# Block-sparse attention with a SwiGLU layer: the loads of batches 1 to 3 on GpSimd's queue, the first query tile on ScalarE, mask columns in two pieces

## The chip, the cores and the metric

The kernel runs on one core of a Trainium2 chip. The metric is the device time of one execution in microseconds (us). A separate execution is taken with the hardware profiler; its page and its trace are what is read here. On the page PE is TensorE's matmul, PEld its weight load, DVE is VectorE, ACT ScalarE, POOL GpSimd and SP SyncE; a letter q behind a name means the engine's sequencer, which waits and issues DMAs. PS is the PSUM tile with its eight banks.

## The reference

Attention over 4 batches, 8 heads, 768 positions and head size 64, with a mask on blocks of 32 positions, followed by a normalised SwiGLU layer on the 3072 x 512 result:

```python
scores = scale * np.matmul(q, k.transpose(0, 1, 3, 2))
mask = np.abs(blk_i - blk_j) <= window          # window = 1
mask = mask | (blk_i == 0) | (blk_j == 0) | (blk_i == n_blocks - 1) | (blk_j == n_blocks - 1)
# and three sampled key blocks for each query block
scores = np.where(mask, scores, -1000000000.0)
attn = softmax(scores)
attn_out = np.matmul(attn, v)
x = attn_out.transpose(0, 2, 1, 3).reshape(B * S, H * D)
rms = np.sqrt(np.mean(x * x, axis=-1, keepdims=True) + 1e-06)
xn = x / rms * rms_g
g = xn @ w_gate                                 # 512 x 1536
silu = g * (1.0 / (1.0 + np.exp(-g)))
val = xn @ w_val
return silu * val @ w_out                       # 1536 x 512
```

Inputs and output are float32.

## The kernel before

**Pairs of heads.** Two heads of one batch are a pair; there are 16 pairs, numbered g, four to a batch. For a pair, k, q and v are loaded as float32, 128 partitions x 2 heads x 384 elements (384 KB each), into a tile `qkv` of which there are three (`raw`). `fill` casts k and q to bf16 into `aug`, 64 columns of each row, beside 24 columns that hold the mask: the keys' block indicator, and for queries the mask row of the query's block. One matmul over 88 rows thus gives scores and mask together. `pad_v` casts v into `vaug`, and with that the pair's `raw` buffer is free again. The transposed form of `aug` goes to `XA`, with five slots: for the four pairs of batch 0 by TensorE (`tpx`, evicted by `evx`), for all later pairs by a DMA transpose, `turn` (L241), from one of two `aug` buffers.

**Units.** The work on queries comes in ten units: three single tiles of 128 queries and one of three tiles for batch 0, then two of three tiles for each further batch. A unit runs QK (`qk`, L272), the exponential on ScalarE (`exp`, L292), AV (`av`, L306), normalisation (`xo`), the sum of squares (`sq`), its reciprocal root on GpSimd (`rsq`, L339), the scaled row (`xq`, L346) and its transpose, by TensorE for the first three units and by a DMA transpose (`xt`, L372) for the others. Then follow gate and value products (`proj`, L384), tanh (`th`, L393), `uu` (L399) and `hp` (L410) on VectorE, and the output product (`yy`, L423), with its eviction `yo` (L433) and the store. While attention of one unit runs, products of an earlier one are put between its matmuls.

**Order.** A planner at the end of the kernel writes all engines' orders. Each step is an `op` with a price for every engine that could run it, its dependences, its priority and the buffers that it takes and gives back. The planner takes in turn the step that could start first by its own clock. Two resources, `DMA` and `DMA2`, stand for SyncE's and ScalarE's queues; a landing is put some time after the issue (8.0 for a load of batches 1 to 3). The engines then run these orders as they stand, each in order, and wait on semaphores.

**Transfers.** Loads of batch 0 are issued at the start, on SyncE's queue except for the first 64 columns of q, which go on ScalarE's. The weights are read as float32 and written as bf16 by DMAs on GpSimd's queue (`load_w`, L207, eight of 128 x 4 x 384; `load_wo`, L211, two of 128 x 6 x 512), behind a small copy that waits for v of pair 1 (`gate_pool`). The loads of batches 1 to 3 are on SyncE's queue, as are the transposes and the stores. Ahead of the loads of pairs 4 to 7, SyncE issues a read of two elements out of a weight tile into `scr` (`gate_sync`, L217); it has to wait until that weight DMA has landed, and what stands behind it in SyncE's order waits too.

**The first query tile.** GpSimd casts the first 64 columns of q for both heads into `aug[0]` (`fillq(0, 0, 1)`), and ScalarE copies all mask columns for queries out of PSUM (L187).

Of the kernel before, what the change touches and what calls it, by code (L numbers as in the profile page):

```python
# [10 lines left out]
BF16 = mybir.dt.bfloat16  # L11
# [6 lines left out]
def kernel(  # L18
# [12 lines left out]
    nc = tc.nc  # L31
    SIMOUT = None
    P = 128
    B, H, S, D = q.shape
    NB = S // 32
    NC = S // P
    DM = H * D
    DFF = moe_w_gate.shape[1]
    NF = DFF // P
    NP = H // 2  # L40
# [3 lines left out]
    KQ = D + NB  # L44
# [12 lines left out]
    const = ctx.enter_context(tc.tile_pool(name="const", bufs=1))  # L57
# [8 lines left out]
    qv = q.rearrange("b h (p c) d -> b p h (c d)", c=NC)  # L66
    kv = k.rearrange("b h (p c) d -> b p h (c d)", c=NC)
    vv = v.rearrange("b h (p c) d -> b p h (c d)", c=NC)

    raws = {}  # L70
    aug = [const.tile([P, 2, 2, NC, P], BF16, name=f"aug{i}") for i in range(NAUG)]
# [4 lines left out]
    def load(g, i):  # L76
        b, pr = divmod(g, NP)
        if i == 0:
            raws[g] = raw.tile([P, 3, 2, NC * D], FP32, name="qkv", tag="qkv")
        nc.sync.dma_start(out=raws[g][:, i], in_=(kv, qv, vv)[i][b, :, 2 * pr:2 * pr + 2, :])  # L80

    TI = work.tile([P, DM], I32, name="ti", tag="yo", bufs=3)
    TF = work.tile([P, DM], FP32, name="tf", tag="yo", bufs=3)
# [6 lines left out]
    A = [raw.tile([P, 3, 2, NC * D], FP32, name="qkv", tag="qkv") for g in range(3)]  # L90
# [9 lines left out]
    load0(1, 0)  # L100
    load0(1, 1)
    gB = const.tile([P, DM], FP32, name="gB")
    scr = const.tile([P, 16], BF16, name="scr")
    scf = const.tile([P, 1], FP32, name="scf")

    def copy(eng, out, in_):
# [19 lines left out]
    def idle(n, bk=7):  # L126
# [7 lines left out]
        out=kmask, in_=kmask, compare_op=ALU.is_ge, fill=0.0,  # L134
        base=0, pattern=[[1, NC], [-32, NB]], channel_multiplier=NC)
    nc.gpsimd.affine_select(
        out=kmask, in_=kmask, compare_op=ALU.is_ge, fill=0.0,
        base=31, pattern=[[-1, NC], [32, NB]], channel_multiplier=-NC)
    nc.gpsimd.affine_select(
        out=ident, in_=ident, compare_op=ALU.not_equal, fill=1.0,  # L140
        base=0, pattern=[[-1, P]], channel_multiplier=1)
    nc.gpsimd.affine_select(
        out=Bm, in_=Bm, compare_op=ALU.is_ge, fill=0.0,
        base=1, pattern=[[-1, 32]], channel_multiplier=1)
    nc.gpsimd.affine_select(
        out=Bm, in_=Bm, compare_op=ALU.is_ge, fill=0.0,
        base=1, pattern=[[1, 32]], channel_multiplier=-1)
    nc.gpsimd.affine_select(
        out=Bm, in_=Bm, compare_op=ALU.not_equal, fill=1.0,
# [13 lines left out]
    for t in aug:  # L163
# [7 lines left out]
        out=eq[0:NB], in0=jb[0:NB], in1=samp_f[0:NB].unsqueeze(2).to_broadcast([NB, NRND, 32]),  # L171
        op=ALU.is_equal)
# [3 lines left out]
    for r in range(NRND):  # L176
        nc.vector.tensor_tensor(
            out=Bm[0:NB], in0=Bm[0:NB], in1=eq[0:NB, r], op=ALU.max)
    nc.vector.tensor_scalar(
        out=Bneg, in0=Bm, scalar1=-MASKV, scalar2=MASKV, op0=ALU.mult, op1=ALU.add)  # L180
    qm = PS[:, 2, 0:NC * NB].rearrange("p (c j) -> p c j", j=NB)
    for c in range(NC):
        nc.tensor.matmul(  # L183
            out=qm[:, c, :], lhsT=Kind[0:NB, c, :], rhs=Bneg[0:NB, 0:NB], start=True, stop=True)
    idle(WARM[2])

    nc.scalar.copy(out=aug[0][:, 1, :, :, D:KQ], in_=qm.unsqueeze(1).to_broadcast([P, 2, NC, NB]))  # L187

    def fillk(g, eng, e=slice(0, 2)):
        copy(eng, aug[g % NAUG][:, 0, e, :, 0:D],  # L190
# [6 lines left out]
    wv = const.tile([P, DM // P, DFF], BF16, name="wv")  # L197
    wo = const.tile([P, NF, DM], BF16, name="wo")
# [3 lines left out]
    NWC, NOC = 4, 2  # L202
    FW, FO = DFF // NWC, NF // NOC
# [6 lines left out]
    def load_wo(i):  # L210
        nc.gpsimd.dma_start(  # L211
            out=wo[:, i * FO:(i + 1) * FO, :], in_=wov[:, i * FO:(i + 1) * FO, :])

    def gate_sync(n):
        f0 = n * FW if n < NWC else (n - NWC) * FO * DM
        src = wv[0:1, 0, f0:f0 + 2] if n < NWC else wo[0:1, (n - NWC) * FO, 0:2]
        nc.sync.dma_start(out=scr[0:1, 2 * n:2 * n + 2], in_=src)  # L217

    def fillq(g, lo, hi, eng):
        src = A[g][:, 1, :, lo * D:hi * D] if lo < 3 else tiles["q2"][:, 2 * g:2 * g + 2, :]  # L220
        copy(eng, aug[g % NAUG][:, 1, :, lo:hi, 0:D], src.rearrange("p e (c d) -> p e c d", d=D))
# [232 lines left out]
    def op(key, engs, deps, prio, fn, acq=(), rel=(), at=0.0):  # L454
        o = dict(key=key, engs=engs, deps=deps, prio=prio, fn=fn, acq=acq, rel=rel, at=at,
                 n=len(ops))
        ops.append(o)
        made[key] = o
# [12 lines left out]
        "p (i e x) -> p i e x", i=3, e=2))  # L471

    ld0(("l", 0, 0), 1.2)
    op(("l", 0, 1, 0), {"DMA2": 0.3}, [], (0,), None)
    ld0(("l", 0, 1, 1), 0.35)
    ld0(("l", 1, 0), 1.0)
    ld0(("l", 1, 1), 0.6)
    for g, i in ((2, 0), (2, 1), (3, 0), (3, 1), (0, 2), (1, 2), (2, 2), (3, 2)):
        ld0(("l", g, i), 0.6 if i == 1 else 1.1,
            lambda e, p, g=g, i=i: load0(g, i))  # L480
    ld0(("lg",), 0.7, lambda e, p: nc.sync.dma_start(
        out=gB, in_=moe_rms_g.unsqueeze(0).to_broadcast([P, DM])))
# [31 lines left out]
    for g in range(NP):  # L514
        a_ = g % NAUG
        rr = [("raw", g)] if g < NP - 1 else []
        if g:
            op(("fk", g), {"DVE": 0.57, "POOL": 0.84}, [("l", g, 0)], (-1, g, 0),
               lambda e, p, g=g: fillk(g, e), [(f"aK{a_}", g)], rr)
        for n_, (es, lo, hi) in enumerate(QP[g == 0]):  # L520
            dep = ("q2",) if lo == 3 else ("l", 0, 1, n_) if g == 0 else ("l", g, 1)
            pri = (-1, g, 1) if lo == 0 else (2.5, g, lo)
            fe = {"DVE": 0.09 + 0.085 * (hi - lo), "POOL": 0.1 + 0.13 * (hi - lo)}
            op(("fq", g, lo), {"POOL": 0.25} if g == 0 and lo == 0 else fe, [dep] + [("m1",)] * (g == 1 and lo == 0), pri,
               lambda e, p, a=(g, lo, hi): fillq(*a, e), [(f"a{'QR'[lo == 3]}{a_}", (g, lo == 3))],
               rr if lo < 3 else [("hp", ("q2",))])
        for i in range(2):
            for n_, (es, lo, hi) in enumerate((KP, QP)[i][g == 0]):
                m_ = len(es) * (hi - lo)
                if i == 0:  # L530
                    pri = (-1, g, 0.5 + 0.1 * n_ + (g == 0 and lo == 3))
                else:
                    pri = (-1, g, 1) if lo == 0 else (2.5, g, lo)
                res = f"aK{a_}" if i == 0 else f"a{'QR'[lo == 3]}{a_}"
                key = ("tp", g, i, es[0], lo)
                op(key, {"PE": m_ * 0.056}, [("fq", g, lo)] if i else [("fk", g)] if g else [],
                   pri, lambda e, p, a=(g, i, es, lo, hi): tpx(*a, p),
                   [(TP1[:2] if i and lo == 3 else TP1, key), (f"X{g}", g)],
                   [(res, g)] if i == 0 else [(res, (g, lo == 3))])
                de = {"DVE": 0.07 + m_ * P / 1560.0}  # L540
                ac = {"ACT": 0.15 + m_ * P / 1200.0}
                if g == 0 and i == 0:
                    de = (de, de, {**de, **ac})[n_]
                elif g == 0 and lo == 0:
                    de.update(ac)
                op(("ev",) + key[1:], de, [key], pri,
                   lambda e, p, a=(g, i, es, lo, hi): evx(*a, e), [], [(None, key)])
        op(("pv", g), {"DVE": 0.57, "POOL": 1.0}, [("l", g, 2)], (0, g, 2),
           lambda e, p, g=g: pad_v(g, e), [("va0", 0)], rr)
# [7 lines left out]
    for g in range(NP, B * NP):  # L557
        b, pr = divmod(g, NP)
        gate = {NP: 2, NP + 1: 3, NP + 2: 4, NP + 3: 5}.get(g)
        for i in range(3):  # L560
            def ld(e, p, g=g, i=i, gate=gate):
                if gate is not None and i == 0:
                    gate_sync(gate)
                load(g, i)
            op(("ld", g, i), {"DMA": 1.1}, [("w", gate)] if gate is not None and i == 0 else [],
               (1,), ld, [("raw", g)] if i == 0 else [])
            if i < 2:
                op(("fill", g, i), {"DVE": 0.57}, [("ld", g, i), ("zp", 0), ("zp", 1)] + [
                    ("tp", g_, i_, 0, 3 * i_) for g_ in (2, 3) for i_ in range(2)],
                   (4, g, i), lambda e, p, g=g, i=i: fill(g, i, e), [(f"aug{g % NAUG}", (g, False))])  # L570
            else:
                op(("pv", g), {"DVE": 0.57}, [("ld", g, 2), ("fill", g, 0), ("fill", g, 1)],
                   (4, g, 2), lambda e, p, g=g: pad_v(g, e), [(f"va{b % 2}", b)], [("raw", g)])
        op(("turn", g), {"DMA": 4.6}, [("fill", g, 0), ("fill", g, 1)], (-1, g),
           lambda e, p, g=g: turn(g), [(f"X{g % NSLOT}", g)], [(f"aug{g % NAUG}", (g, False))])
# [11 lines left out]
    for u, (b, c0, nt) in enumerate(UNITS):  # L587
# [32 lines left out]
        if u < NPET:  # L620
            op(("tr", u), {"PE": nt * NP * 0.056}, [("xq", u, t) for t in range(nt)], (0, u),
               lambda e, p, u=u: tr(u, p), [(TP1 if nt < 3 else S_, ("tr", u)), ("xn", u)], [("xq", u)])
            op(("cp", u), {"ACT": 0.15 + nt * DM / 1200.0, "DVE": 0.17 + nt * DM / 1950.0}, [("tr", u)], (0, u),
               lambda e, p, u=u: cp(u, e), [], [(None, ("tr", u))])
        else:
            op(("cp", u), {"DMA": 1.8}, [("xq", u, t) for t in range(nt)], (-2, u),
               lambda e, p, u=u: xt(u), [("xn", u)], [("xq", u)])
        fg = FG[nt]
        w_of = [-(-(f + 1) * fg * P // FW) - 1 for f in range(NF // fg)]
# [25 lines left out]
                op(("yo", u, t, h), {"ACT": 0.15 + DM / nh / 1200, "DVE": 0.16 + DM / nh / 960}, [("y", u, t, 4 * h + 3)], (5, u, t),  # L655
                   lambda e, p, a=(u, t, h): yo(*a, e), [], [(None, ("y", u, t, h))])

    free = {"PE": 4.7, "ACT": 4.98, "DVE": 4.7, "POOL": 3.2, "DMA": 2.1, "DMA2": 2.3}
    left = {o["key"]: len(o["deps"]) for o in ops}
    users = {}  # L660
    for o in ops:
# [37 lines left out]
    while ready:  # L699
# [22 lines left out]
        _, o, e, t1, got = pick  # L722
# [73 lines left out]
```

The softmax here doesn't subtract the row's maximum and nothing guards it: scores larger than these inputs give would overflow.

## Time and profile before

| What | Value |
|---|---|
| Median of 3 runs | 309.65 us (309.52 to 312.66) |
| The profiled execution's own time | 309.14 us |
| Its span, first to last instruction | 307.4 us |
| TensorE busy | 299.2 us, 97% |
| ScalarE busy | 202.4 us, 66% |
| VectorE busy | 192.1 us, 62% |
| GpSimd busy | 25.1 us, 8% |
| DMA on SyncE's queue | 37.56 MB, 48.9% of 16 engines' span |
| DMA on GpSimd's queue | 4.72 MB (as written), 9.9% |
| Loads of k, q, v: issue to landing, median | 5.5, 6.0, 5.6 us |
| Weights: wg, wv, wo, the same | 7.1, 8.2, 18.4 us |
| DMA transposes to XA and xn, the same | 6.5, 4.4 us |

Busy time of TensorE is modelled from the starts of its matmuls. A group's line has its source line, engine and operation, output and inputs by the program's names, the count, the busy time and the mean, and the idle time of the engine just before it with what ended most of that. A line of the waits has who waited for whom, the total, the count and the longest. A line of a timeline has the start and the length in us.

### The profile page before, as it was taken

What the parts mean: (1) busy time and instruction counts of PE and PEld (TensorE: products, weight loads), DVE (VectorE), ACT (ScalarE), POOL (GpSimd) and SP (SyncE); (2) the same over time, 40 slices, a digit from 0 to 9 for tenths busy, and PEclk for the clock granted to TensorE, in tenths of its full rate; (3) what the DMA queues carried; (4) which work ended last, traced back from release to release, by engine and by line L of the source; (5) the groups of instructions that cost most, each with busy time, mean ns of one, the idle gap of its engine ahead of it and who ended that gap; (6) DMA issues with size and microseconds to landing.
All of it is one profiled execution on the core that took longest, in us unless ns stands there. A gap on an engine that the chain in (4) does not pass through costs nothing.

```text
span 307.4 us, 7325 instructions
## 1 busy us (share of the span) xinstructions
PE 299.2 (97%) x3022; PEld 199.6 (65%) x3050; DVE 192.1 (62%) x434; ACT 202.4 (66%) x317; POOL 25.1 (8%) x44
## 2 busy tenths in 40 slices
PE   8999999989999999999999999999999999999995
PEld 7898888746667566666666666666666556556543
DVE  6778766855779768756754754663499617627500
ACT  4999875676887888777778787888723223333221
POOL 4566000100000001001000100010001000000000
PEclk9999999999999999999999999999999999999999
DMA  7999999999999899940793050003100140020022
GB/s 213 365 224 190 225 277 214 225 301 275 264 272 249 229 208 267 267 151 16 148 189 81 0 87 2 34 3 85 36 0 2 23 132 2 11 91 2 0 104 104
DMA packets 72230, 42.82 MB, mean 139 GB/s; under 512 B 49924, under 2 KB 69124, under 8 KB 72196
## 3 DMA queue, kind: packets, MB, share of 16 engines
q1 hardware_dynamic: 66096, 37.56, 48.9%
q0 software_dynamic: 5792, 4.72, 9.9%
q8 instruction: 24, 0.39, 0.5%
q10 hardware_dynamic: 308, 0.07, 0.1%
q14 instruction: 10, 0.08, 0.1%
HBM read 28.57 MB, written 6.29 MB: 113 GB/s over the span
## 4 chain that ended last, share of the span: by engine, by line
PE 95%; ACT 2%; DMA 2%; issue 1%; DVE 0%; ACTq 0%
PE PS L384 41%; PE PS L272 19%; PE PS L423 19%; PE PS L306 12%; PE PS L254 2%; DMA xn<-xq 2%; ACT pt L292 1%; PE PS L128 1%; PE PS L153 0%; PE PS L357 0%; ACT yo L433 0%; PE PS L183 0%; DVE zt L115 0%; ACTq L433 0%
## 5 line engine op out<-in xcount | busy, mean ns | idle before, releaser
L292 ACT ACTIVATE pt<-PS 128x768 bf16<-128x768 f32 x188 | 142.9, 812 | 33.7 <-PE PS L272 33.2
L399 DVE SCALAR_TENSOR_TENSOR uu<-th,PS 128x384 bf16<-128x384 bf16 x96 | 53.1, 554 | 61.7 <-ACT th L393 58.8
L272 PE MATMUL PS<-XA 88*128 88x384 bf16 (+1 forms) x480 | 81.7, 294 | 0.6 <-ACT pt L292 0.6
L384 PE MATMUL PS<-xn,wg 128*128 128x384 bf16 (+1 forms) x480 | 75.2, 294 | 1.2 <-DMA xn<-xq 1.2
L384 PE MATMUL PS<-xn,wv 128*128 128x384 bf16 (+1 forms) x480 | 75.3, 293 | 0.0
L393 ACT ACTIVATE th<-PS 128x384 bf16<-128x384 f32 x96 | 47.3, 493 | 38.1 <-PE PS L384 35.4
L423 PE MATMUL PS<-wo,hp 128*128 128x512 bf16 (+1 forms) x272 | 65.5, 370 | 1.5
L410 DVE TENSOR_TENSOR hp<-uu,PS 128x384 bf16<-128x384 bf16 x96 | 51.4, 551 | 15.2 <-PE PS L384 14.6
L384 PEld LDWEIGHTS <-wg 128*128 128x128 bf16 x480 | 41.4, 98 | 23.9 <-issue 1.6
L384 PEld LDWEIGHTS <-wv 128*128 128x128 bf16 x480 | 41.6, 97 | 23.4
L272 PEld LDWEIGHTS <-XA 88*128 88x128 bf16 x480 | 39.4, 98 | 21.3 <-issue 1.6
L423 PEld LDWEIGHTS <-hp 128*128 128x128 bf16 x300 | 29.0, 98 | 26.8
L306 PEld LDWEIGHTS <-pt 128*128 128x128 bf16 x1128 | 40.5, 97 | 5.7
L306 PE MATMUL PS<-vaug,pt 128*128 128x65 bf16 x1128 | 42.1, 193 | 0.0
L433 ACT ACTIVATE yo<-PS 128x512 f32<-128x512 f32 (+1 forms) x23 | 13.3, 580 | 26.4 <-PE PS L423 25.7
L339 POOL TENSOR_TENSOR rs<-ms,nhalf 128x3 f32<-128x3 f32 (+1 forms) x10 | 7.9, 786 | 204.0 <-DVE ms L331 163.7
L318 DVE TENSOR_TENSOR xo<-PS,rz 128x384 f32<-128x384 f32 (+1 forms) x40 | 19.1, 477 | 1.4
L346 DVE SCALAR_TENSOR_TENSOR xq<-xo,rs,gB 128x512 bf16<-128x512 f32 x24 | 17.5, 748 | 3.3 <-POOL rs L339 3.3
L331 DVE CUSTOM_DVE_ANT_0 sc<-xo 128x512 bf16<-128x512 f32 (+1 forms) x24 | 16.3, 680 | 0.2
L112 DVE CAST aug<-qkv 128x768 bf16<-128x768 f32 (+1 forms) x28 | 14.5, 538 | 0.1
L317 DVE RECIPROCAL rz<-PS 128x6 f32<-128x6 f32 (+1 forms) x40 | 7.4, 186 | 8.1 <-PE PS L306 7.8
L112 DVE COPY XA<-PS 88x768 bf16<-88x768 bf16 (+2 forms) x17 | 8.5, 518 | 2.7 <-PE PS L254 2.7
(59 smaller groups left out, 71.2 us busy)
## 6 DMA issues: line engine op xcount, KB each, us to landing
out_dram<-yo SPq DMA_DIRECT2D x23, 256.0 KB, 2.2
qkv<-in_v_dram SPq DMA_DIRECT2D x15, 384.0 KB, 5.6
qkv<-in_k_dram SPq DMA_DIRECT2D x14, 384.0 KB, 5.5
qkv<-in_q_dram SPq DMA_DIRECT2D x12, 384.0 KB, 6.0
wg<-in_moe_w_gate_dram POOLq DMA_DIRECT2D x4, 384.0 KB, 7.1
wv<-in_moe_w_val_dram POOLq DMA_DIRECT2D x4, 384.0 KB, 8.2
wo<-in_moe_w_out_dram POOLq DMA_DIRECT2D x2, 768.0 KB, 18.4
q<-in_q_dram SPq DMA_DIRECT2D x1, 768.0 KB
```

The lines of the kernel that those rows point to most:

```text
L112: nc.vector.tensor_copy(out=out, in_=in_)
L272: nc.tensor.matmul(out=s_[:, e, j * w:(j + 1) * w], lhsT=x[0:KQ, 0, e, jt * P:(jt + 1) * P], rhs=x[0:KQ, 1, e, c0 * P:c0 * P + w], start=T ...
L292: nc.scalar.activation(out=pts[u, pr][:, g * kt:(g + 1) * kt].rearrange("p j e w -> p e j w"), in_=s_[:, :, 0:kt * w].rearrange("p e (j w) ...
L306: nc.tensor.matmul(out=o_[:, t, e, :], lhsT=pt[:, jt, e, t * P:(t + 1) * P], rhs=va[:, (2 * pr + e) * NC + jt, 0:D + 1], start=(jt == 0), ...
L318: nc.vector.tensor_tensor(out=xos[u][:, :, 2 * pr:2 * pr + 2, :], in0=o_[:, :, :, 0:D], in1=rz.unsqueeze(3).to_broadcast([P, nt, 2, D]), o ...
L331: nc.vector.tensor_tensor_reduce(out=sc[:, z], in0=x, in1=x, scale=1.0 / DM, scalar=mss[u][:, 0:1] if nt == 1 and t else 1e-6, op0=ALU.mul ...
L346: nc.vector.scalar_tensor_tensor(out=xqs[u][:, t, :], in0=xos[u][:, t].rearrange("p h d -> p (h d)"), scalar=mss[u][:, t:t + 1], in1=gB, o ...
L384: nc.tensor.matmul(out=p_[:, j, :].rearrange("p (t w) -> p t w", w=P), lhsT=w_[:, c, f_ * P:(f_ + 1) * P], rhs=xns[u][:, :, c, :], start=( ...
L393: nc.scalar.activation(out=t_, in_=tiles["gp", u, f], func=AF.Tanh, scale=0.5)
L399: nc.vector.scalar_tensor_tensor(out=t_, in0=tiles.pop(("th", u, f)), scalar=1.0, in1=tiles.pop(("gp", u, f)), op0=ALU.add, op1=ALU.mult)
L410: nc.vector.tensor_tensor(out=hps[u][:, f * fg:(f + 1) * fg, :], in0=tiles.pop(("uu", u, f)), in1=tiles.pop(("vp", u, f)), op=ALU.mult)
L423: nc.tensor.matmul(out=tiles["yp", u, t, h], lhsT=hps[u][:, f, t * P:(t + 1) * P], rhs=wo[:, f, x], start=(f == 0), stop=(f == NF - 1))
```

## The change

The loads of batches 1 to 3 are issued by GpSimd, behind the weights in its order, and the first of them also behind the reciprocal root of unit 2. `gate_sync` and `scr` are gone. ScalarE casts the first query tile, in place of GpSimd, ahead of its copy of the mask columns, and that copy is made in two pieces: the first tile's columns, then the other five tiles'. Four prices of the planner change with it: a load costs 0.9 on GpSimd in place of 1.1 on SyncE, a transpose of `xq` 2.6 in place of 1.8, the first load on ScalarE's queue 0.1 in place of 0.3, and ScalarE is taken to be free at 4.84 in place of 4.98.

```diff
-        nc.sync.dma_start(out=raws[g][:, i], in_=(kv, qv, vv)[i][b, :, 2 * pr:2 * pr + 2, :])
+        nc.gpsimd.dma_start(out=raws[g][:, i], in_=(kv, qv, vv)[i][b, :, 2 * pr:2 * pr + 2, :])
...
-    scr = const.tile([P, 16], BF16, name="scr")
...
-    nc.scalar.copy(out=aug[0][:, 1, :, :, D:KQ], in_=qm.unsqueeze(1).to_broadcast([P, 2, NC, NB]))
+    nc.scalar.copy(
+        out=aug[0][:, 1, :, 0, 0:D], in_=A[0][:, 1, :, 0:D])
+    for c in (slice(0, 1), slice(1, NC)):
+        nc.scalar.copy(out=aug[0][:, 1, :, c, D:KQ],
+                       in_=qm[:, c].unsqueeze(1).to_broadcast([P, 2, c.stop - c.start, NB]))
...
-    def gate_sync(n):
-        f0 = n * FW if n < NWC else (n - NWC) * FO * DM
-        src = wv[0:1, 0, f0:f0 + 2] if n < NWC else wo[0:1, (n - NWC) * FO, 0:2]
-        nc.sync.dma_start(out=scr[0:1, 2 * n:2 * n + 2], in_=src)
...
-    op(("l", 0, 1, 0), {"DMA2": 0.3}, [], (0,), None)
+    op(("l", 0, 1, 0), {"DMA2": 0.1}, [], (0,), None)
...
-            op(("fq", g, lo), {"POOL": 0.25} if g == 0 and lo == 0 else fe, [dep] + [("m1",)] * (g == 1 and lo == 0), pri,
-               lambda e, p, a=(g, lo, hi): fillq(*a, e), [(f"a{'QR'[lo == 3]}{a_}", (g, lo == 3))],
+            op(("fq", g, lo), {"ACT": 0.001} if g == 0 and lo == 0 else fe, [dep] + [("m1",)] * (g == 1 and lo == 0), pri,
+               None if g == 0 and lo == 0 else lambda e, p, a=(g, lo, hi): fillq(*a, e), [(f"a{'QR'[lo == 3]}{a_}", (g, lo == 3))],
...
             def ld(e, p, g=g, i=i, gate=gate):
-                if gate is not None and i == 0:
-                    gate_sync(gate)
                 load(g, i)
-            op(("ld", g, i), {"DMA": 1.1}, [("w", gate)] if gate is not None and i == 0 else [],
+            op(("ld", g, i), {"POOL": 0.9}, ([("w", gate)] if gate is not None and i == 0 else []) + [("rsq", 2)] * (g == NP),
                (1,), ld, [("raw", g)] if i == 0 else [])
...
-            op(("cp", u), {"DMA": 1.8}, [("xq", u, t) for t in range(nt)], (-2, u),
+            op(("cp", u), {"DMA": 2.6}, [("xq", u, t) for t in range(nt)], (-2, u),
...
-    free = {"PE": 4.7, "ACT": 4.98, "DVE": 4.7, "POOL": 3.2, "DMA": 2.1, "DMA2": 2.3}
+    free = {"PE": 4.7, "ACT": 4.84, "DVE": 4.7, "POOL": 3.2, "DMA": 2.1, "DMA2": 2.3}
```

What the planner makes of it: TensorE's order is the same up to about 50 us and has its groups in another order after that. The first QK of pair 4 and all that hangs on it stand earlier in it. On SyncE 44 rows are left of 85, and GpSimd has 79 in place of 42.

## The prediction

> **What bounds the kernel now.** I read the busy shares first, then the chain, then the waits of TensorE, then the DMA by stage, and last the two queues that the change rearranges.
>
> ```profile
> PE 299.2 (97%) x3022; PEld 199.6 (65%) x3050; DVE 192.1 (62%) x434; ACT 202.4 (66%) x317; POOL 25.1 (8%) x44
> ...
> PE 95%; ACT 2%; DMA 2%; issue 1%; DVE 0%; ACTq 0%
> ```
>
> TensorE is busy 97% and is 95% of the chain that ended last. The orders of the two programs hold the same 3050 matmuls, 38 idle ones among them in both, so that work can't shrink. What is left is 307.4 - 299.2 = 8.2 us of idle time. The waits of TensorE say where a part of it is:
>
> ```profile
> PE PS L384 <- DMA xn<-xq: 1.2, 1, 1.2
> PE PS L128 <- DVE zt L115: 1.1, 1, 1.1
> PE PS L272 <- ACT pt L292: 0.6, 2, 0.3
> ```
>
> 1.1 us is the very start, and about 4 us stand after the last matmul (the timeline has them end near 303.6 of 307.4); neither is touched. The one large wait inside is 1.2 us at 69.40, for the transposed xn of unit 3. So the change can win little, and it can lose as much as a late transfer costs. DMA is the resource to look at. Three stages, each as its GB/s slices or queue shares say: 18 to 34 us (weights alone), 36 to 44 (weights beside loads), and SyncE's timeline:
>
> ```profile
> DMA packets 4094, 3.11 MB, mean 195 GB/s; under 512 B 126, under 2 KB 4091, under 8 KB 4091
> q0 software_dynamic: 4084, 3.07, 127.8%
> ...
> q0 software_dynamic: 875, 0.88, 64.7%
> q1 hardware_dynamic: 853, 1.24, 50.2%
> ...
> 31.39 0.75 SPq L217 DMA_DIRECT2D scr<-wv  x1
> ...
> 32.32 0.40 SPq L80 DMA_DIRECT2D qkv<-in_k_dram  x1
> ...
> 45.78 10.27 SPq L241 DMA_TRANSPOSE XA<-aug  x2
> ...
> 64.65 2.58 SPq L372 DMA_TRANSPOSE xn<-xq  x1
> ```
>
> Weights (counted in bf16 as written) come at 195 GB/s alone. Once the loads of pair 4 start, the two queues take turns: 875 packets against 853 in 8 us. The DMA digits of the page stand at 9 to about 42% of the span; the engines are full there, so what goes first decides what is late.
>
> **What the Trainium skill says.** "DMA: Bandwidth & Descriptors", section "Queues, rings and completion order": each DMA engine goes round its queues packet by packet. The section "SWDGE vs HWDGE vs iDMA" puts a packet at preferably up to 4096 B and at most 64 descriptors, and says that GpSimd's DMAs have one queue; the paragraph on issuing engines there says that all of them end on the same 16 engines. The trace agrees on the turns (875 to 853). At 49 us, on an engine that still has weights, packets of the two queues alternate singly (weight, load, weight, every 152 ns), while the 256-byte rows of the first query load on ScalarE's queue ran 16 in a row, 14 ns apart, though SyncE's queue had work. "SBUF — State Buffer", section "Who interferes with whom": VectorE's copies in a two-port mode lock GpSimd out, so its descriptors are late. The trace bounds that: weight issues took 0.74 to 0.95 us beside a busy VectorE.
>
> **The change part by part.** All times are on the clock of the profiled execution, 309.14 us (span 307.4 and 1.7 around it), 0.5 us below the median of 309.65.
>
> *Start.* The query fill of GpSimd (0.70 us, 4.21 to 4.91) goes to ScalarE, which is free until the mask matmuls end (it waits 0.64 us before L187). ScalarE then copies 128x128, 128x48 and 128x240 instead of 128x288 (0.40 us at 4.64). By the 0.37 us that it takes for 256 elements (L108), the three are about 0.25, 0.2 and 0.37; the first lies in its wait, the second ends near 4.85 where the old one ended at 5.04. The first query tile needs no more than these two. Gain up to 0.2 us, taken as 0.2; no loss over 0.2, since the third piece serves later tiles.
>
> *Gates gone.* Four 4-byte reads and 36 loads leave SyncE. Its transposes and outputs no longer stand behind loads. The xn transpose of unit 3 waited behind an output at 64.20 and was issued at 64.65, 1.6 us after its last xq (60.94 + 2.07 = 63.0); in the new order only a turn stands before it, and the planner now allows 2.6 instead of 1.8 for it. I take 1.0 of the 1.2 us at 69.40 as won; bounds 0 and 1.2.
>
> *Loads behind the weights.* 36 issues on GpSimd at 0.75 us are 27 us on an engine busy 25; between 32 and 130 us it has room. Each load of a fourth or later pair waits for its raw buffer, and the reciprocal roots (L339) stand behind such loads; but a root's own input comes later than that buffer's release in VectorE's order, so I cost this at 0, and up to 1 us if v of pair 8 is late.
> One queue is first in, first out. The third pair of weight chunks landed at 29.4 and 31.4 (issued 22.44 and 23.68, 7.0 and 7.7 to landing), so one chunk is 1.95 us. Two more chunks and two output halves of 3.9 give 31.4 + 3.9 + 7.8 = 43.1 for the last weight (49.9 before, where loads took every second packet). A load of 393 KB at 370 GB/s (alone, near 83 us) is 1.07. So k, q, v of pair 4 land at 44.1, 45.2, 46.3; k and q of pair 5 at 47.3 and 48.4. Before, k and q of pair 4 landed at 39.7 and 42.9.
> VectorE's order is shared up to the product that ran at 42.62. After it the new one has: fill k4, fill q4, hp, pad v4, uu, fill k5, rz, xo, hp, fill q5, uu, hp, pad v5, uu, fill k6, rz, xo, hp. It ran this before:
>
> ```profile
> 42.62 0.55 DVE L410 TENSOR_TENSOR hp<-uu,PS 128x384 bf16<-128x384 bf16 x1 [0.25 <-PE PS L384]
> 43.09 0.55 DVE L112 CAST aug<-qkv 128x768 bf16<-128x768 f32 x1
> ...
> 51.92 0.56 DVE L399 SCALAR_TENSOR_TENSOR uu<-th,PS 128x384 bf16<-128x384 bf16 x1 [0.71 <-ACT th L393]
> ...
> 53.87 0.54 DVE L410 TENSOR_TENSOR hp<-uu,PS 128x384 bf16<-128x384 bf16 x1
> ```
>
> Fill q4 thus waits from 43.6 to 45.2, and hp behind it ends at 46.3 instead of 45.2. TensorE's next value group starts at 46.86, so this is hidden, barely.
>
> *The turn of pair 4.* It is issued at about 45.8, as before (45.78), and its packets start 1.2 us later, at 47.0. It has 786 KB in 3072 packets of 256 B; at 217 GB/s (alone, near 150 us) 3.6 us. If it drains 16 packets (224 ns) for each load packet (65 ns), it has 0.78 of the engines: 4.6 us, landing near 52.3 with the 0.6 us that the next turn showed from last packet to landing. The first QK of pair 4 ran at 56.95; the new matmul order has 4.0 us less work before it (summed over both orders with the pitches of the rows), so it is due at 53.0. Cost 0, with 0.7 us to spare.
> *What the turns push back.* k6 is the seventh load: 43.1 + 7 x 1.07 + 3.6 = 54.2, and about 1.5 more since the turn of pair 5 (issued near 51) takes three quarters of the engines at its end: 55.7. Fill k6 is due between 51.92 and 53.17, at about 52.5. The hp behind it ends at 55.7 + 0.5 + 0.7 + 0.5 = 57.4 instead of 54.4, 3 us late. TensorE waits for that product's bank; its reserve there is about 1 us (0.5 before the group at 54.95, 1.6 at 46.86). Cost 2.0, bounds 0 (k6 in time) and 3.
>
> **Sum.** -0.2 - 1.0 + 2.0 = +0.8: 309.14 + 0.8 = 309.9 on the profiled clock, 310.4 against the median.
>
> **Rivals.**
> (1) The turn does not get whole runs of packets but alternates one for one. Seven or eight loads (v5 to v7) stand queued at 47.0, 16 packets on each engine: 128 x 79 ns = 10.1 us, then the turn's other 64 alone, 0.9: landing at 58.6 against a need of 53.0, a stall of 5.6, and 1 to 2 more at the next turns: 316.5. For it: single alternation of weights and loads. Against: the 16 in a row on ScalarE's queue. It decides from a share of the turn under 0.67 (3.6 us within 5.4), and makes over 1% under about 0.4.
> (2) Loads are slower on GpSimd's queue, by late descriptors or by one slow engine (in 47 to 50 us one still had weights when the rest had none). At 1.25 instead of 1.07, k6 is 1.3 later and the backlog reaches the fills of pairs 8 and 9 as well: 2 + 1.3 + about 2 = 314.
> (3) Only waits go, the landings hold: -1.2, or 308.4. Against it: pair 4 lands 4 us later than before by the sum above.
> (4) The change does not do what it says: the ungated loads were gated by the queue's own order anyway, so SyncE's relief is all. The result is that of (3).
>
> **How the numbers follow.** Forecast case 0.45 (309 to 312.5), (1) 0.20, (2) 0.18, (3) and (4) 0.17. 1% of 309.65 is 3.1 us, about what a measurement of this kernel can tell from no change. Slower: (1), most of (2) and a tail of the forecast, 0.40. Faster by over 1% would need more than the 1.4 us that I can find: 0.05. Same 0.55. The range reaches from (3) less 0.4 to (1) with its next stalls, 308.0 to 317.5; the likeliest case's own is 309 to 312.5.
>
> **What would show it.** Right: the wait for xn near 69 gone, VectorE idle at 43.6 and at about 53 before a cast of aug for a DMA of qkv, TensorE waiting some 2 us near 56 on L384, pair 4's first QK without a wait. Wrong: a wait of TensorE on L272 for XA near 53 (rival 1), casts that wait at 70 to 80 (rival 2), or a wait-free 40 to 70 (rival 3).

## The result, and the profile after

| | Before | After |
|---|---|---|
| Median, us | 309.58 (309.37 to 312.66, 4 runs) | 344.73 (341.30 to 351.07, 4 runs) |
| Profiled execution, us | 309.14 | 347.12 |
| Its span, us | 307.4 | 345.4 |

The ratio after to before is 1.103, with an interval of 1.094 to 1.112. The forecast of 310.4, with a range of 308.0 to 317.5, is far off. Some executions run a few per cent longer at a lower granted clock, for the changed kernel three of six with the profiled one among them, so the ratio and the comparisons below use its other three, 341.30, 342.34 and 342.76. With 342.34 the change costs 32.8 us; of the 38 us by which the profiled execution is longer than the one before some 5 are its own.

Busy shares, granted clock and chain on the page of the changed kernel:

```profile
PE 305.5 (88%) x3021; PEld 202.7 (59%) x3050; DVE 194.2 (56%) x438; ACT 200.5 (58%) x315; POOL 50.6 (15%) x79
...
PEclk9999997579967859999999999999999999999999
...
q1 hardware_dynamic: 56288, 23.40, 32.3%
q0 software_dynamic: 9824, 18.88, 23.8%
...
PE 72%; DMA 24%; DVE 2%; issue 1%; POOL 0%; SPq 0%; ACT 0%; DVEq 0%; POOLq 0%; ACTq 0%
```

The chain has gone from 95% TensorE to 72%, with 24% DMA. TensorE's idle time is 345.4 - 305.5 = 39.9 us, against 8.2 before: 31.7 more. Its busy time is 6.3 more for the same matmuls: the clock digits drop as low as 5 where it stands, and four matmuls of QK just after a stall take 1.46 us (below) where such a group took 0.81 before. 31.7 + 6.3 is the whole difference of 38.0 in span. Its waits, and the three places where it stands, on its timeline:

```profile
PE PS L270 <- DMA XA<-aug: 24.7, 2, 16.1
PE PS L382 <- DVE hp L408: 8.0, 1, 8.0
```

```profile
69.45 1.46 PE L270 MATMUL PS<-XA 88*128 88x384 bf16 x4 [16.11 <-DMA XA<-aug]
103.63 1.46 PE L270 MATMUL PS<-XA 88*128 88x384 bf16 x4 [8.56 <-DMA XA<-aug]
122.53 1.44 PE L382 MATMUL PS<-xn,wv 128*128 128x384 bf16 x4 [8.05 <-DVE hp L408]
```

Before, the first QK of pair 4 was

```profile
56.95 0.81 PE L272 MATMUL PS<-XA 88*128 88x384 bf16 x4
```

The wait for xn is gone, and 32.7 us of waits for turns, or for what hangs on them, stand in its place (in the new file QK is L270, the products L382, `turn` L239). VectorE stands for the same turns, since a fill needs the `aug` buffer that the turn still reads. The longest of these waits ends at 69.50; another, of 10.2 us, ends at 119.86, and TensorE's third stall waits for an `hp` behind it. Among the waits of VectorE:

```profile
DVE aug L111 <- DMA XA<-aug: 37.8, 4, 16.8
```

No such wait comes after 123 us, though loads land until 159: from there on they come three at a time, and turns land 5.5 to 9.3 us after issue. Two answers for the time of the first stall: transfers of 50.2 to 69.5 us, and busy times with DMA share and GB/s in two stretches.

```profile
DMA packets 4646, 3.60 MB, mean 186 GB/s; under 512 B 4002, under 2 KB 4120, under 8 KB 4645
...
q1 hardware_dynamic: 3884, 0.99, 64.5%
q0 software_dynamic: 761, 2.60, 51.2%
```

```profile
47.00:50.00 3.00, 3.00 (x43) 2.55 (x43) 2.83 (x8) 2.85 (x5) 2.51 (x3) 1.00 1.02 369
50.00:69.40 19.40, 3.29 (x55) 2.49 (x54) 1.51 (x3) 1.70 (x3) 2.16 (x3) 0.67 1.16 187
```

From 47 to 50 the loads run alone at 369 GB/s. From 50 on, with the turn of pair 4 under way, the engines are as full (1.02 and 1.16), but move only half as much; a turn alone moved some 217 in the kernel before. The turn was issued at 45.8 and landed 23.6 us later, near 69.4.

### The profile page after: what moved, and what is told of

Read it like the earlier page. It is cut to its first block, busy times and chain, and to the rows that moved or that the text cites. A ratio compares the mean times of both kernels' runs of the same rounds, so it can differ in the third digit from the quotient of the medians.

```text
span 345.4 us, 7325 instructions
## 1 busy us (share of the span) xinstructions
PE 305.5 (88%) x3021; PEld 202.7 (59%) x3050; DVE 194.2 (56%) x438; ACT 200.5 (58%) x315; POOL 50.6 (15%) x79
## 3 DMA queue, kind: packets, MB, share of 16 engines
HBM read 28.57 MB, written 6.29 MB: 101 GB/s over the span
## 4 chain that ended last, share of the span: by engine, by line
PE 72%; DMA 24%; DVE 2%; issue 1%; POOL 0%; SPq 0%; ACT 0%; DVEq 0%; POOLq 0%; ACTq 0%
PE PS L382 32%; DMA XA<-aug 17%; PE PS L421 16%; PE PS L270 14%; PE PS L304 8%; DMA qkv<-in_q_dram 5%; DMA qkv<-in_v_dram 2%; PE PS L252 0%; DVE aug L111 0%; DVE vaug L111 0%; SPq L93 0%; POOL qkv L80 0%; DVE sc L329 0%; DVE xo L316 0%; DVE hp L408 0%
## 5 line engine op out<-in xcount | busy, mean ns | idle before, releaser
L270 PE MATMUL PS<-XA 88*128 88x384 bf16 (+1 forms) x480 | 83.0, 299 | 25.2 <-DMA XA<-aug 24.7
L382 PE MATMUL PS<-xn,wv 128*128 128x384 bf16 (+1 forms) x480 | 77.3, 299 | 8.0 <-DVE hp L408 8.0
L382 PE MATMUL PS<-xn,wg 128*128 128x384 bf16 (+1 forms) x480 | 77.1, 299 | 0.0
L270 PEld LDWEIGHTS <-XA 88*128 88x128 bf16 x480 | 39.8, 99 | 47.2 <-DMA XA<-aug 24.9
L382 PEld LDWEIGHTS <-wv 128*128 128x128 bf16 x480 | 42.6, 99 | 32.4 <-issue 9.7
L382 PEld LDWEIGHTS <-wg 128*128 128x128 bf16 x480 | 42.5, 100 | 23.7 <-issue 1.4
L304 PEld LDWEIGHTS <-pt 128*128 128x128 bf16 x1128 | 41.4, 99 | 6.0 <-issue 0.7
L304 PE MATMUL PS<-vaug,pt 128*128 128x65 bf16 x1128 | 42.9, 195 | 0.3 <-DVE xo L316 0.3
L111 DVE CAST aug<-qkv 128x768 bf16<-128x768 f32 (+1 forms) x28 | 14.6, 542 | 39.4 <-DMA XA<-aug 37.8
L431 ACT ACTIVATE yo<-PS 128x512 f32<-128x512 f32 (+1 forms) x19 | 11.0, 577 | 27.7 <-PE PS L421 27.3
L316 DVE TENSOR_TENSOR xo<-PS,rz 128x384 f32<-128x384 f32 (+1 forms) x40 | 19.1, 478 | 1.4
L80 POOL DMA_DIRECT2D qkv<-in_k_dram x12 | 9.2, 770 | 59.8 <-DVE vaug L111 57.2
```

What stands on the lines that cost most here:

```text
L111: nc.vector.tensor_copy(out=out, in_=in_)
L270: nc.tensor.matmul(out=s_[:, e, j * w:(j + 1) * w], lhsT=x[0:KQ, 0, e, jt * P:(jt + 1) * P], rhs=x[0:KQ, 1, e, c0 * P:c0 * P + w], start=T ...
L304: nc.tensor.matmul(out=o_[:, t, e, :], lhsT=pt[:, jt, e, t * P:(t + 1) * P], rhs=va[:, (2 * pr + e) * NC + jt, 0:D + 1], start=(jt == 0), ...
L316: nc.vector.tensor_tensor(out=xos[u][:, :, 2 * pr:2 * pr + 2, :], in0=o_[:, :, :, 0:D], in1=rz.unsqueeze(3).to_broadcast([P, nt, 2, D]), o ...
L382: nc.tensor.matmul(out=p_[:, j, :].rearrange("p (t w) -> p t w", w=P), lhsT=w_[:, c, f_ * P:(f_ + 1) * P], rhs=xns[u][:, :, c, :], start=( ...
```

## The experiments

All ratios are to the kernel before, run on the same chip. "Theory A" is that loads on one queue beside turns on another are the whole loss; "theory C" that the planner's new order costs by itself. (In the expectations of e1_sync and e5_wait_turn that order is rival B, and C is loads that are slow on GpSimd's queue in themselves.)

**Loads back on SyncE's queue (e1_sync), then with the gates as well (e7_sync_gates).**

```diff
-        nc.gpsimd.dma_start(out=raws[g][:, i], in_=(kv, qv, vv)[i][b, :, 2 * pr:2 * pr + 2, :])
+        nc.sync.dma_start(out=raws[g][:, i], in_=(kv, qv, vv)[i][b, :, 2 * pr:2 * pr + 2, :])
...
+                if gate is not None and i == 0:      # e7_sync_gates only
+                    gate_sync(gate)
```

> The changed kernel with one word undone: the 36 loads of batches 1 to 3 are issued by SyncE, at the same places of the planner's order, so TensorE, VectorE and ScalarE keep the changed order and nothing gates the loads. Theory A (transposes and loads of two queues wreck each other on the DMA engines): one queue serves them one after the other, the first two turns land 6 to 10 us after their issue instead of 23.6, the 24.7 us of TensorE's waits for XA go, 309 to 312 us. Rival B (the new order is to blame: pair 4's turn is needed 4 us earlier than it can land, and the loads are not gated): the waits stay, above 330 us. Rival C (GpSimd's loads are slow in themselves): about 309 too, so this run parts A and C from B, not A from C.

> The changed kernel with its loads back on SyncE's queue and SyncE's four gate reads ahead of pairs 4 to 7; the planner's order of all other engines, the start part and the price 2.6 stay. Theory A (the loads' queue beside the transposes is the whole loss): waits for XA under 1 us in all, turns land 5 to 8 us after issue, weights again in 6 to 9 us, 309.5 to 312. Theory C (the order that the planner now writes, with pair 4 due at 53, needs landings that no queue gives): TensorE waits 3 us or more near 53 for XA or hp, 314 or above.

e1_sync took 321.52 us, ratio 1.038 (1.035 to 1.041); e7_sync_gates 319.45, ratio 1.033 (1.030 to 1.036). Both missed the 309 to 312 that theory A gave. The waits of TensorE, e1_sync first:

```profile
PE PS L382 <- DMA wg<-in_moe_w_gate_dram: 5.4, 1, 5.4
PE PS L382 <- DVE hp L408: 4.0, 1, 4.0
...
PE PS L270 <- DMA XA<-aug: 0.7, 1, 0.7
```

```profile
PE PS L388 <- DVE hp L414: 5.2, 2, 4.6
PE PS L276 <- DMA XA<-aug: 3.4, 2, 2.2
```

Neither is a clean undo. In e1_sync nothing holds the loads behind the weights (on GpSimd's queue the order did), and TensorE waits for weights. In e7_sync_gates the gates hold them again, but the planner still counts the loads on GpSimd. So SyncE's order has the loads of pair 6 ahead of the turn of pair 4; in one first-in, first-out queue that turn waits its time, and its first QK starts at 56.1 after a wait of 2.2. What both show is the size. By their traces TensorE, VectorE and ScalarE run the very orders of the changed kernel; with loads and turns in one queue these cost 10 to 12 us, with two queues 33. By these two runs about two thirds of the loss come with the second queue. The other third is theory C for this plan on SyncE's queue; how much of it the plan costs on GpSimd's queue is not parted from the rest.

**GpSimd's queue kept, turns held free of loads (e5_wait_turn).** Ahead of the loads of pairs 6, 8, 10, 12 and 14, GpSimd copies one column of the XA slot of the pair ahead of it, so that it goes on only when that turn has landed. The planner is told of this wait, `("turn", g - 1)` among the dependences of the load, and writes its orders anew.

```diff
+                if g >= NP + 2 and g % 2 == 0 and i == 0:
+                    nc.gpsimd.tensor_copy(out=scf, in_=X[(g - 1) % NSLOT][:, 0, 0, 0:1])
                 load(g, i)
```

> The changed kernel with the loads still on GpSimd's queue, but before the loads of pairs 6, 8, 10, 12 and 14 GpSimd copies one column of the XA slot of the pair before, so that two pairs' loads start only when the turns before them have landed (the planner knows of that wait). Loads and turns then overlap little. Theory A: no turn takes over 12 us to land, TensorE's waits for XA shrink from 24.7 us to under 8 (loads come later, so some stay), 311 to 322 us. Rival C (loads slow in themselves on this queue): loads still take 11 us and more though nothing runs beside them, and it stays above 335. Rival B (order): above 335.

311.18 us, ratio 1.005 (1.003 to 1.008): 31.2 of the 32.8 us are back. Its TensorE wait, and the first of the new waits on GpSimd's timeline:

```profile
PE PS L382 <- DMA xn<-xq: 2.0, 1, 2.0
```

```profile
57.33 0.35 POOL L561 CAST scf<-XA 128x1 f32<-128x1 bf16 x1 [20.95 <-DMA XA<-aug]
```

GpSimd stands 21 us for the two turns and issues no load in that time (the last one out before lands at 48.9, the turn is issued at 45.4), no wait for XA is left, and turns land 5.5 to 7.3 us after issue. The loads still go out on GpSimd's queue and behind the weights. So loads on that queue, kept apart from the turns and with a plan that knows it, cost no more than the 1.6 us that remain. The plan is not quite that of the changed kernel: TensorE's order is the same up to 77 us, but in VectorE's the fill of k6 no longer stands ahead of the normalisation at 53. The run shows that keeping loads and turns apart brings the time back; it does not clear the changed kernel's order.

**Which collision (e10_wait_late, e11_wait_first).** The same wait for pairs 8, 10, 12 and 14 only, and for pair 6 only; the lines are against e5_wait_turn, and the planner is told of the same pairs.

```diff
-                if g >= NP + 2 and g % 2 == 0 and i == 0:
+                if g >= NP + 4 and g % 2 == 0 and i == 0:      # e10_wait_late
+                if g == NP + 2 and i == 0:                     # e11_wait_first
```

> The changed kernel in which only the loads of pairs 8, 10, 12 and 14 wait for the turn ahead of them; those of pair 6 are free, so the turns of pairs 4 and 5 again run beside them. If each collision costs by itself: the first stall of the changed kernel stays (turn of pair 4 landing near 69, some 16 us at its first QK), the later two are gone, 326 to 332. If holding later loads is enough because the backlog is what delays the turns: under 318.

> The changed kernel in which only the loads of pair 6 wait for the turn of pair 5; all later ones are free. If each collision costs by itself: pair 4 lands by 54 without a wait of TensorE for it, the stalls near 100 and 120 stay in some form, 322 to 334. If one early delay sets off the later ones: under 316.

e10_wait_late took 323.86 us, ratio 1.045 (1.040 to 1.050), a little under the expected 326 to 332. e11_wait_first took 332.22, within its 322 to 334, in the one execution that can be compared; the other three, the profiled one of 341.01 among them, took 338.09 to 341.01. The TensorE timeline of e10_wait_late:

```profile
66.52 1.46 PE L270 MATMUL PS<-XA 88*128 88x384 bf16 x4 [13.14 <-DMA XA<-aug]
```

and that of e11_wait_first:

```profile
77.21 1.46 PE L382 MATMUL PS<-xn,wg 128*128 128x384 bf16 x4 [7.32 <-DMA xn<-xq]
113.95 1.44 PE L382 MATMUL PS<-xn,wv 128*128 128x384 bf16 x4 [12.74 <-DVE hp L408]
156.75 1.44 PE L382 MATMUL PS<-xn,wg 128*128 128x384 bf16 x4 [5.45 <-DVE uu L397]
```

The first collision alone costs 323.86 - 311.18 = 12.7 us, the later ones alone 332.22 - 311.18 = 21.0, by one execution. Together 33.7, against 342.34 - 311.18 = 31.2 for both at once: each collision costs by itself. In the profiled execution of e11_wait_first the later ones come earlier and fall on the xn transpose as well.

**Another second queue (e2_act).** The loads go out on ScalarE's queue.

> The changed kernel with its loads issued by ScalarE instead of GpSimd, ungated. Theory A (a second queue alone delays a turn to 10 to 15 us, as in the transfers by themselves, and only GpSimd's queue also loses throughput): turns beside loads land 9 to 15 us after issue, waits for XA 4 to 12 us in all; the loads start ahead of the weights too, which costs 5 to 10 us of waits for weights and hp as it did on SyncE, and ScalarE stands for raw buffers: 318 to 332. Theory B (any second queue beside the transposes loses as much): waits for XA 20 us or more, turns of 19 us, 340 or above.

334.86 us, ratio 1.083 (1.079 to 1.088), between the two expectations. TensorE, VectorE and ScalarE again run the orders of the changed kernel. TensorE's waits:

```profile
PE PS L270 <- ACT pt L290: 11.1, 6, 8.1
PE PS L270 <- DMA XA<-aug: 8.7, 1, 8.7
```

The turn of pair 4 lands 19.3 us after issue, so a turn is late beside loads on this queue too. Waits for XA are a third of the changed kernel's, and the rest is ScalarE, whose exponentials stand behind a load; the profile puts the longest of these stands, 8.2 us until 93.2, down to a turn that landed then. The waits for weights that were expected did not come. The late turn is therefore no property of GpSimd's queue alone.

**The transfers by themselves (e6_bench, e9_bench2, e12_bench3).** Phases one after the other, most of the kernel's own shapes, none of the computation. Each phase ran once.

> Only transfers, none of the computation: six phases with a join on VectorE between them, all of one size: two turns of 786 KB and nine loads of 393 KB. Phase 1 two turns alone on SyncE's queue; 2 nine loads alone on GpSimd's; 3 nine loads alone on SyncE's; 4 loads on GpSimd's beside turns on SyncE's; 5 loads on ScalarE's beside turns on SyncE's; 6 loads, then turns, all on SyncE's. Expected from the traces: 1 about 9 us, 2 and 3 about 11 to 12, 6 about 18 to 20 (the sum of the work). Theory A: 4 takes well over the sum, 30 us or more, and in it a 256-byte packet alternates with a load packet of 4608 bytes. Whether 5 does so too is open: if it does, two queues suffice; if it takes about 20, it is GpSimd's queue and its packets. Rival C: 2 takes 20 us or more. If 4 takes about 20 us, A is wrong.

> Transfers alone, none of the computation, seven phases: two plain copies of the same 786 KB in 256-byte rows on SyncE's queue alone; nine loads on GpSimd's queue beside them; four quarters of the gate weights on GpSimd's queue alone, then beside two turns; nine loads in halves of 768 bytes a row on GpSimd's queue beside two turns; three loads on it beside two turns; five loads on it beside four on SyncE's. Theory A1 (it takes transposes and GpSimd's queue together): loads beside plain copies 20 us or less with the sum of both alone as a floor, weights beside turns 5 us above their sum. Theory A2 (it takes GpSimd's packets of several rows beside any small packets): loads beside plain copies 24 us or more; halves lose less if their packets are smaller. Both: three loads beside turns lose 2 us or less over 14; loads beside loads 13 to 14.5 us.

> Transfers alone, none of the computation, six phases: two plain copies in 256-byte rows on GpSimd's queue alone, then beside two turns; nine stores of 384 KB on GpSimd's queue alone, then beside two turns; three loads on ScalarE's queue beside two turns; three loads on GpSimd's queue beside two turns. Two turns alone took 9.3 us. If a turn loses beside reads from memory only: copies and stores beside turns take no more than the sum of both alone, and three loads on either queue 15 to 18 us. If it loses beside anything on GpSimd's queue: copies and stores 4 us or more over the sum, three loads on ScalarE's queue 13 us or less, on GpSimd's 17.

The stretches of e6_bench: two turns alone; nine loads on GpSimd's queue alone; nine on SyncE's alone; nine on GpSimd's beside two turns; on ScalarE's beside two; on SyncE's with two turns behind them. The last two figures of a line are DMA share and GB/s.

```profile
4.00:14.00 10.00, 1.16 (x8) 0.08 (x1) 1.00 0.84 157
14.00:27.00 13.00, 0.00 (x0) 6.51 (x9) 1.00 0.80 272
27.50:41.30 13.80, 0.12 (x4) 0.00 (x0) 1.00 0.76 256
41.80:66.00 24.20, 0.23 (x2) 6.47 (x9) 1.00 1.03 211
66.00:86.00 20.00, 0.49 (x6) 0.00 (x0) 1.00 1.00 256
86.00:105.50 19.50, 0.74 (x8) 0.00 (x0) 1.00 0.97 262
```

The next table has the times from the first issue to the VectorE instruction that waits for the last landing, with the sum of the two alone. Its last column is the time that the packets of the two turns took, per DMA engine: their share of 16 engines times the stretch (in SyncE's phase, that of the 256-byte packets alone).

| Beside two turns | Alone, us | Sum, us | Together, us | Packets of the turns, us |
|---|---|---|---|---|
| nothing | | | 9.3 | 8.4 |
| nine loads, GpSimd's queue | 13.2 | 22.5 | 24.2 | 12.7 |
| nine loads, ScalarE's queue | not measured | | 19.5 | 8.6 |
| nine loads, SyncE's queue | 13.7 | 23.0 | 19.1 | 8.4 |
| weight chunks, GpSimd's queue | not measured | | 20.3 | 9.1 |
| nine loads in halves of 768-byte rows, GpSimd's queue | not measured | | 28.7 | 12.0 |
| three loads, GpSimd's queue (two phases) | not measured | | 17.3, 16.6 | 12.4, 11.8 |
| three loads, ScalarE's queue | not measured | | 13.8 | 8.7 |
| two plain copies in 256-byte rows, GpSimd's queue | 13.4 | 22.7 | 18.1 | 9.2 |
| nine stores, GpSimd's queue | 12.6 | 21.9 | 21.2 | 11.7 |

Without turns: nine loads on GpSimd's queue beside two plain copies on SyncE's took 18.4 (sum 24.0), and five on GpSimd's beside four on SyncE's 12.0. The sums with copies are too high as a measure, since of two copies alone the second waits for the first.

The phase of the weights is not four chunks against their sum. VectorE waits there for the first chunk only, 5.2 us, and three chunks of the phase before are still moving when the turns start: GpSimd's queue moved 2.49 MB beside them, where four chunks are 1.57. Whether weights cost more than their work beside turns was therefore not tested.

Several expectations missed: 24.2 where 30 or more was expected; halves took more, not less; three loads on GpSimd's took 17.3 in e9_bench2 where 16 at most was expected, and on ScalarE's lost nothing where one theory gave 15 to 18; loads beside loads took 12.0 where 13 to 14.5 was. What stands is two things. First, a turn beside loads of another queue is late, on either queue: the first one landed 14.5 us after issue with nine loads on GpSimd's and 14.6 with nine on ScalarE's, against 5.8 alone. Behind nine loads in its own queue it landed 10.1 us after its issue, but 15.5 after the first load's: here one queue brought it no sooner. In the kernel the gain of one queue is that loads issued behind a turn cannot go ahead of it; in the changed kernel six did (below). Second, some traffic on GpSimd's queue stretches the turns' own packets as well: from 8.4 us to between 11.7 and 12.7 with loads and with stores, but only to 9.2 with copies inside SBUF and to 9.1 with weights, and to 8.7 at most with loads on the other two queues. In all, nine loads took 4.7 us longer on this queue than on ScalarE's, three loads 3.5 and 2.8. The loads and stores had packets of 3072 and 4608 bytes for the most part, the copies of 4096 and the weights of 1024; what it is about the former stays open.

**The start by itself, and the price by itself (e3_start, e8_xt_only).** The kernel before with only the new start; the kernel before with only the new price:

```diff
-            op(("cp", u), {"DMA": 1.8}, [("xq", u, t) for t in range(nt)], (-2, u),
+            op(("cp", u), {"DMA": 2.6}, [("xq", u, t) for t in range(nt)], (-2, u),
```

> The kernel before with only the start of the change: ScalarE casts the first query tile, the mask columns go in two pieces, ScalarE is taken to be free at 4.84 and the first load on its queue costs 0.1 in the plan. The loads stay on SyncE behind their gates. The prediction put this at 0.2 us of gain: 309.4 against 309.6. If the start had a part in the 35 us, this would show it; I expect between 309.0 and 309.8.

> The kernel before with one edit, the planner's price of a transpose of xq 2.6 in place of 1.8. If the price makes the planner issue or place it so that the wait for xn near 69 goes: that wait 0 to 0.3 us in place of 1.2, no other wait of more than 0.5, 308.2 to 309.2. If the wait depends on SyncE being full of loads there, not on the price: 1 to 2 us of wait for xn as before, 309.2 to 310.2.

e3_start: 310.03 us, ratio 1.0019 (1.0007 to 1.0031), 0.6 slower. e8_xt_only: 308.68 against 309.46, ratio 0.9981 (0.9967 to 0.9994), 0.8 us less and the only version here that beats the kernel before, by 0.2%. Their waits for xn, e3_start first:

```profile
PE PS L388 <- DMA xn<-xq: 1.8, 2, 1.7
```

```profile
PE PS L384 <- DMA xn<-xq: 0.3, 1, 0.3
```

The start moves the first QK from 6.29 to 6.02 us in e3_start, but by 8.2 TensorE has waited 0.2 for a cast and is level with before, and the order that follows puts 0.6 us more on xn. The price takes 0.9 us of that wait away, as was expected of it; its profiled execution has another wait of 0.8 us, for a cast at 8.28, where no other over 0.5 was expected.

## Why the prediction was wrong

**The step that failed** is "The turn of pair 4", cost 0 "with 0.7 us to spare". The trace gives its terms:
- The packets' start. Predicted 47.0, 1.2 us after the issue. The first packet of the turn is at 50.03 in the changed kernel, 47.07 before, 46.69 in e5_wait_turn; it is as late with loads on ScalarE's queue (50.14 in e2_act). Where 3 us went between issue and packet is not settled; loads filled the engines in that time.
- The share. "16 packets (224 ns) for each load packet (65 ns)" was wrong in both numbers. On GpSimd's queue loads travel in packets of 4608 bytes, three rows in one, 188 ns each; on SyncE's they had been single rows of 1536. And the turn does not get runs of 16: near 58 us, as far as the packets of one engine can be told apart, load packets follow each other every 200 ns or so with one 256-byte packet (18 ns) between them. From 50 to 66 us the turn has 1899 packets against 637 of loads with data, three to one, so it gets more than one at a time on some engines or at some times. The run of 16 that was taken for proof was ScalarE's 256-byte rows beside SyncE's loads, not a transpose. "DMA: Bandwidth & Descriptors" of the Trainium skill, section "Queues, rings and completion order", has an engine drain "a whole packet" before it switches, and a packet of typically 9 to 17 descriptors; what the trace records as a packet of the turn is one row.
- So all eight loads that had yet to land at 50.3, q6 to v8, landed ahead of the turn, the last at 68.2, though six of them were issued after it. Their work is 8 x 1.07 = 8.6 us. With 3.6 for the turn and 0.6 to its landing that gives 62.8.
- The throughput. It landed at 69.4. The missing 6.6 us are lost throughput, 187 GB/s where loads alone had moved 369 and a turn alone 217, a loss that the prediction had no term for.

The turn also had a second user that the prediction left out: VectorE's fill of k6 needs its `aug` buffer, and stood 16.81 us for it.

**Rival 1 was the nearest, mis-sized.** It named single alternation (seen near 58 us, not all along), the wait on L272 for XA and the place near 53, and gave 58.6 and 316.5. It had 1536-byte packets of loads that were all queued at 47, no late start, no lost throughput. Its "1 to 2 more at the next turns" was 16.6 us of stalls (8.6 at 95.1 and 8.0 at 114.5): the turn issued at 84.6 ran beside eight loads and took 19.0 us to land. Chance 0.20 was too low for something that the trace had shown between weights and loads.

**Nor was the clock in the sum.** TensorE's busy time grew by 6.3 us. In the page's slices the granted clock is 5 to 8 tenths around the stalls. "TensorE: Matmul & The Clock Gate" of the Trainium skill, "Part 1: The HAM clock gate", says that an idle TensorE falls to half its clock; this trace agrees, with 0.50 from 60 to 70 us, inside the first stall. A stall of 16 us thus costs more than 16: the work after it starts at a lower clock, 0.82 on the mean of 70 to 80.

**Steps that held.** The first in, first out sum for GpSimd's queue was right to 0.2 us for five landings, predicted 44.1, 45.2, 46.3, 47.3 and 48.4, and 44.0, 45.1, 46.1, 47.2 and 48.2 in the trace. VectorE's timeline shows the casts that take the first three:

```profile
44.02 0.56 DVE L111 CAST aug<-qkv 128x768 bf16<-128x768 f32 x1 [0.62 <-DMA qkv<-in_k_dram]
45.07 0.56 DVE L111 CAST aug<-qkv 128x768 bf16<-128x768 f32 x1 [0.49 <-DMA qkv<-in_q_dram]
46.12 0.56 DVE L111 CAST vaug<-qkv 128x768 bf16<-128x768 f32 x1
```

The turn was issued at 45.78 (45.8 predicted), pair 4 was due at 53.3 (69.45 - 16.11; 53.0 predicted), and the wait for xn went. k6 was predicted at 55.7 behind the turn; it landed at 50.3, ahead of it, so the 2.0 us for a late k6 never came; its fill waited for the turn instead.

**The start** was costed at -0.2 and came out at +0.6 by e3_start. In the changed kernel its first QK is at 6.13 instead of 6.29, as predicted, but a gain at one place is not one at the end where a list of orders is drawn up anew after it.

**Rivals 2 to 4.** Loads are not slower on GpSimd's queue as such: 13.2 us for nine, 13.7 on SyncE's. The landings did not hold: k of pair 4 landed at 44.0 against 39.7 before, as the prediction had it. No wait of TensorE came of that before 53 us, and with turns and loads held apart e5_wait_turn took 311.2, still 2.8 above rival 3's 308.4.

**What stays open:** how loads or stores on GpSimd's queue and a transpose take throughput from each other; how much the changed kernel's order costs on that queue; why the turn's packets started 3 us late; and why ScalarE's queue, which lost no throughput beside turns by themselves, still had a turn of 19.3 us in the whole kernel.

## What to carry to other kernels

Before moving transfers to another queue, list what they will newly run beside. One queue is also a schedule: in it a short urgent transfer waits for what is ahead of it (15.5 us where nine loads were), and in two queues it shares the engines with everything that is on the other, what is issued after it included. Count the share by packets of that very kind of transfer on that very queue, and where a transpose is on the path, hold bulk loads back until it has landed; the kernel with that wait on the little used GpSimd was 1.6 us above the kernel before, the one without it 32.8.

## What the runs showed of the hardware

- Loads of 1536-byte rows are sent in packets of 4608 bytes (188 ns) on GpSimd's queue and of 1536 bytes (65 ns) on SyncE's and ScalarE's.
- Beside DMA transposes, load packets of GpSimd's queue were at times recorded with 2 us and more each, against 188 ns alone; the transfers together moved 187 GB/s in the kernel, against 369 for loads alone there, and 211 in e6_bench, against 256 with the loads on ScalarE's queue.
- Two turns beside nine loads: 24.2 us with the loads on GpSimd's queue, 19.5 on ScalarE's, 19.1 on SyncE's; the turns' packets took 12.7, 8.6 and 8.4 us per engine.
- In a TensorE stall of 16.1 us the granted clock fell to 0.50, and was 0.82 on the mean of the 10 us after it; three stalls of 32.7 us in all came with 6.3 us more of busy time.
